# An mLSTM cell and a leaky-ReLU layer in one kernel: weight conversion spread over three engines, a second buffer for exp(a), and a reordered first stage

## The chip, the cores and the metric

The kernel runs on one core of a Trainium2 chip. A core has five instruction streams that run side by side: TensorE (PE in the profile, with its weight loads as PEld), VectorE (DVE), ScalarE (ACT), GpSimd (POOL) and SyncE (SP). SP issues nearly all the DMAs here; ACT issues the few that load the gates. Each stream runs its instructions in order and waits on semaphores for the others. The metric is the device time of one execution in microseconds (us); lower is better.

## The reference, cut to what matters

The first half is a recurrent cell per batch and head (4 x 8 heads, 768 steps, 40 values per head); its output feeds two dense layers with a leaky ReLU between them.

```python
for t in range(S):                                   # S = 768
    m_new  = maximum(f[t] + m, i[t])
    f_stab = exp(f[t] + m - m_new);  i_stab = exp(i[t] - m_new);  m = m_new
    C = f_stab * C + i_stab * outer(v[t], k[t]);     n = f_stab * n + i_stab * k[t]
    y[t] = sigmoid(o[t]) * (C @ q[t]) / maximum(abs(n @ q[t]), 1)
x = y.transpose(0, 2, 1, 3).reshape(3072, 320)
h = x @ w_in                                         # 320 x 2048
out = maximum(0.01 * h, h) @ w_out                   # 2048 x 320
```

Both weight matrices arrive as float64, because the generator scales them by a numpy float64. The other inputs are float32.

## The kernel before, in words

**Chunks and steps.** The 768 time steps are cut into 6 chunks of 128 (NB = 6). A *step* s = 4c + b is one chunk c of one batch b, all 8 heads: 24 steps. Inside a chunk the recurrence is done in matrix form: scores k.q times a decay matrix exp(a[t] + b[s]) below the diagonal, and the state C carries what came before. The dense layers of chunk c, for the 512 tokens of its four batches, are the *ff* work of chunk c.

**A cell step in pieces.** `feed` (L652) loads k and v and spreads the vector a over all partitions into a tile `w` (four buffers), and exp(a) into a tile `ea` (one buffer, L329). `load_blocks` (L306) loads k, q and o a second time into `rb`, laid out for 32x32 transposes. `ahead(s)` (L640) prepares step s: `prep_kq` (transposes of k and q on DVE, L403, and q times exp(a), L409), the loads of k and q for step s + 2, `prep_mask` (POOL adds the causal mask to `w`, L357), `prep_exp` (ACT, eight exps, L365), `prep_vu` (POOL, L384), `prep_o` (ACT, tanh of half the output gate, L392). `u_scores` (L428) is the score matmul and its product with `w` (DVE, L436). `u_mix` (L498) computes the output: matmuls into `pT` (L507, L513), then on DVE a transpose `hb` (L519), the denominators and `xb` (L523), POOL L526, DVE L530, and four DMAs to a scratch `x_dr` in DRAM (L533). `gather_x` (L536) reads it back, transposed, as `xT`, the input of the dense layers.

**The ff work.** `ff_units` gives a list of units: matmuls `ph` (L576) with the relu on ACT (L584) into `acts`, then matmuls `po` (L611), summed over all of `w_out`, with an output copy and DMA. Both `ph` and `po` come out of one pool of four PSUM buffers, so at most two pairs of `ph` are open at once.

**Weights.** The float64 weights come in eight pieces of 1.25 MiB, four of `w_in` and four of `w_out` (QN = 4): `load_weights(n)` (L169) loads piece n into one of two raw buffers (piece 0 into columns of `acts` that are not in use yet), and the generator `narrow_weights(n)` (L197) turns it into float32: an absolute value of the high words on ACT (L209), and on DVE a clamp (L211), an and with a shift (L215), sign and exponent put together (L219), the exponent alone (L221), low word times 2^-52 times that exponent (L223), and a sum (L227). Each `yield` is a place where other work may go in between.

**Order.** PE, DVE, ACT and POOL run in exactly the order in which the program emits their instructions. SP's queue is ordered by the planner of the Tile framework, which follows program order except where it expects a buffer not to be free yet. `first_chunk` (L656) does the cell of chunk 0 and starts the ff work of chunk 0. Then for c = 1 to 6 a loop (L753) runs the ff units of chunk c - 1 and puts the nine cell units of chunk c between them (`u_scores` and `u_mix` for four steps, and `u_gates`, the transposed gates of the next chunk). In pass c = 1 there are 30 ff units, i = 0 to 29: fourteen `ph` units, then sixteen `po` units in which every four need one more piece of `w_out`. There the loop also converts pieces 2 to 7: `todo` (L751) names the unit at which a conversion starts, and each unit then advances it by two yields. The line that places the cell units is

```python
upto = min(n_c, max(0, i + 1 - lead) * n_c // (n_ff - 6 - lead))
```

with lead = 10 in pass 1 and 0 later. In pass 1 that puts `u_scores`, `u_mix`, ... behind units 11, 13, 14, 16, 17, 19, (gates) 20, 22 and 23.

Of the kernel before, what the change touches and what calls it, by code (L numbers as in the profile page):

```python
# [9 lines left out]
F32 = mybir.dt.float32  # L10
# [8 lines left out]
def kernel(  # L19
# [76 lines left out]

    ident = consts.tile([P, P], F32, name="ident")
    make_identity(nc, ident[:])
    zeros = consts.tile([P, P], F32, name="zeros")
    nc.vector.memset(zeros[:], 0.0)  # L100


# [8 lines left out]

    NL = 4
    NR = 2
    kq_t = [consts.tile([P, 2, H, DP], F32, name=f"kq{n}") for n in range(NL)]
    va_t = [consts.tile([P, H, DP], F32, name=f"va{n}") for n in range(NL)]
    rb_t = [consts.tile([P, 3, RW], F32, name=f"rb{n}") for n in range(NR)]
# [52 lines left out]
    def load_weights(n):  # L169

        if n < QN:
            dst = w_in[:, n, :]
        else:
            dst = w_out[:, 4 * (n - QN) : 4 * (n - QN + 1), :].rearrange("p a d -> p (a d)")
        to = dst
        if wide:
            if n == 0:
                raw = acts_l[:, NF * GT - 2 * WC :].bitcast(U64)
            else:
                raw = wk.tile([P, dst.shape[1]], U64, name="raw")[:]  # L180
            raws[n] = (raw, dst)
            to = raw
        if n < QN:
            for r in range(2):
                cols = slice(n * QC + 2 * P * r, n * QC + 2 * P * (r + 1))
                src = moe_w_in[:, cols].rearrange("(k p) c -> p k c", p=DP)
                half = to[DP * r : DP * (r + 1), :].rearrange("p (k c) -> p k c", k=KC)
                at = 0
                while at < KC:
                    k0, n_k = run_of(r, at)  # L190
                    nc.sync.dma_start(half[:, at : at + n_k, :], src[:, k0 : k0 + 2 * n_k - 1 : 2, :])
                    at += n_k
        else:
            rows = moe_w_out[(n - QN) * QC : (n - QN + 1) * QC, :]
            nc.sync.dma_start(to.rearrange("p (a d) -> p a d", d=Dm), rows.rearrange("(a p) d -> p a d", p=P))

    def narrow_weights(n):  # L197

        if not wide:
            return
        raw, dst = raws.pop(n)
        words = raw.bitcast(U32).rearrange("p (c two) -> p c two", two=2)
        lo, hi = words[:, :, 0], words[:, :, 1]
        mt = wk.tile([P, dst.shape[1]], U32, name="wm", bufs=1)
        m = mt[:]
        d = dst.bitcast(U32)
        nc.scalar.activation(dst, hi.bitcast(F32), AF.Abs)  # L209

        nc.vector.tensor_scalar(  # L211
            m.bitcast(F32), dst, scalar1=2.0**-15, scalar2=122879.9921875, op0=ALU.max, op1=ALU.min,
        )
        yield
        nc.vector.tensor_scalar(  # L215
            m, m, scalar1=0x07FFFFFF, scalar2=3, op0=ALU.bitwise_and, op1=ALU.logical_shift_left,
        )
        yield
        nc.vector.scalar_tensor_tensor(d, in0=hi, scalar=0xC0000000, in1=m, op0=ALU.bitwise_and, op1=ALU.bitwise_or)  # L219
        yield  # L220
        nc.vector.tensor_scalar(m, d, scalar1=0xFF800000, scalar2=None, op0=ALU.bitwise_and)  # L221
        yield
        nc.vector.scalar_tensor_tensor(  # L223
            m.bitcast(F32), in0=lo, scalar=2.0**-52, in1=m.bitcast(F32), op0=ALU.mult, op1=ALU.mult,
        )
        yield
        nc.vector.tensor_tensor(dst, dst, m.bitcast(F32), op=ALU.add)  # L227
        yield


    a_dr = dr.tile([NB, 2, BH, P], F32, name="a_dr")
# [4 lines left out]
    def gates(c):  # L236


        m0 = m0s.get(c)
        n = P if c == 0 else BH  # L240
        fc, il = (f0[:], i0[:]) if c == 0 else (fi[c][:, 0, :], fi[c][:, 1, :])
        F = wk.tile([n, P], F32, name="F", bufs=1)
        nc.vector.tensor_tensor_scan(F[:], fc, zeros[:n], 0.0, op0=ALU.add, op1=ALU.add)
        if c > 0:
            il_t = wk.tile([BH, P], F32, name="il", bufs=1)
            nc.vector.tensor_scalar(il_t[:], il, scalar1=m0[:], scalar2=None, op0=ALU.subtract)
            il = il_t[:]
        m = wk.tile([n, P], F32, name="m", bufs=1)
        nc.vector.tensor_tensor_scan(m[:], fc, il, -1e30 if c == 0 else 0.0, op0=ALU.add, op1=ALU.max)
        a = wk.tile([n, P], F32, name="a", bufs=1)  # L250
        nc.vector.tensor_tensor(a[:], F[:], m[:], op=ALU.subtract)
        if c > 0:
            nc.sync.dma_start(a_dr[c, 0], a[:])
        bu = wk.tile([BH, 3, P], F32, name="bu", bufs=1)
        nc.vector.tensor_tensor(bu[:, 0, :], il[:BH], F[:BH], op=ALU.subtract)
        nc.scalar.activation(bu[:, 1, :], bu[:, 0, :], AF.Exp, bias=a[:BH, P - 1 :], scale=1.0)
        nc.scalar.activation(bu[:, 2, :], a[:BH], AF.Exp)
        if c > 0:
            nc.sync.dma_start(a_dr[c, 1], bu[:, 2, :])
            if c + 2 < NB:  # L260
                load_fi(c + 2)
        if c + 1 < NB:
            m1 = wk.tile([BH, 1], F32, name="m0")
            if c == 0:
                nc.vector.tensor_copy(m1[:], m[:BH, P - 1 :])
            else:
                nc.vector.tensor_tensor(m1[:], m0[:], m[:, P - 1 :], op=ALU.add)
            m0s[c + 1] = m1
        return bu, a
# [27 lines left out]

    def load_o(s):
        c, b = divmod(s, B)
        at = NF * GT - 2 * WC - (s + 1) * Dm  # L300
        st[s]["o"] = acts_l[:, at : at + Dm]
        nc.sync.dma_start(
            st[s]["o"].rearrange("p (h d) -> p h d", d=D), o_gate[b, :, ts(c, P), :].rearrange("h p d -> p h d"),
        )
# [18 lines left out]
    def spread(s):  # L323

        c, b = divmod(s, B)
        d = st[s]
        d["w"] = wk.tile([P, H, P], F32, name="w", bufs=NL)
        nc.sync.dma_start(d["w"][:], a_dr[c, 0, b * H : (b + 1) * H, :].partition_broadcast(P))
        d["ea"] = wk.tile([P, PR, P], F32, name="ea", bufs=1)  # L329
        for r in range(2):  # L330
            nc.sync.dma_start(
                d["ea"][DP * r : DP * (r + 1)], a_dr[c, 1, b * H + r : (b + 1) * H : 2, :].partition_broadcast(DP),
            )
# [164 lines left out]
    def u_mix(s):  # L498

        c, b = divmod(s, B)  # L500
        d = st[s]
        if c + 1 < NB:
            state(s)
        pT = psc.tile([P, PR * P], F32, name="pT", tag="c")
# [135 lines left out]
    def ahead(s):  # L640

        if s < NS:
            prep_kq(s)
            if s + NR < NS:
                load_blocks(s + NR, 0)
                load_blocks(s + NR, 1)
            prep_mask(s)
            prep_exp(s)
            prep_vu(s)
            prep_o(s)  # L650

    def feed(s):  # L652
        load(s)
# [80 lines left out]
    with tc.manual_schedule(engines={E.PE, E.DVE, E.Activation, E.Pool}):  # L734
        ffs = first_chunk()
        feed(B)
        for i in range(3):
            load_blocks(B, i)
        load_weights(QN)
        load_weights(QN + 1)  # L740
        feed(B + 1)
        for i in range(3):
            load_blocks(B + 1, i)
        load_weights(QN + 2)
        load_weights(QN + 3)
        feed(B + 2)
        feed(B + 3)


        ffs = ffs[4:6] + ffs[2:4] + ffs[6:]  # L750
        todo = {0: 2, 4: 3, **{9 + 4 * n: QN + n for n in range(4)}}  # L751
        now = iter(())
        for c in range(1, NB + 1):  # L753
            if c > 1:
                ffs = ff_units(c - 1)
            cells = cell_units(c) if c < NB else []
            n_ff, n_c = len(ffs), len(cells)
            lead = 10 if c == 1 else 0
            done = 0
            waiting = []  # L760
            for i in range(n_ff):
                if c == 1:
                    if i in todo:
                        for _ in now:
                            pass
                        now = narrow_weights(todo[i])
                    next(now, None)
                    next(now, None)
                    if i == 8:
                        u_gates(1)  # L770
                        ahead(B)
                if i == lead and c + 1 < NB:
                    bus[c + 1] = gates(c + 1)
                ffs[i]()
                upto = min(n_c, max(0, i + 1 - lead) * n_c // (n_ff - 6 - lead))
                while done < upto:
                    fn, s = cells[done]
                    fn(s)
                    done += 1
                    if fn is u_scores:  # L780
                        ahead(s + 1)
                    elif fn is u_mix:
                        waiting.append(s)
                        if s + NR < NS:
                            load_blocks(s + NR, 2)
                        if s + NL < NS:
                            feed(s + NL)
                if i >= n_ff // 2 - 1:
                    for s in waiting:
                        gather_x(s)  # L790
                    waiting.clear()


# [29 lines left out]
```

## Time and profile before

| What | Value |
|---|---|
| median of 16 runs | 611.89 us (605.89 to 615.09) |
| the profiled execution, its own time | 610.87 us |
| its span, first to last instruction | 609.1 us |
| PE busy | 543.7 us, 89% of the span |
| PEld busy | 369.3 us, 61% |
| DVE busy | 257.2 us, 42% |
| ACT busy | 154.9 us, 25% |
| POOL busy | 110.8 us, 18% |
| mean granted TensorE clock | 0.958 |

Stretches of the span, from the trace: chunk 0 and the start of its ff work run to about 62 us; pass c = 1 from there to 190.8 us; passes 2 to 5 end at about 279, 366, 454 and 537 us; pass 6, which has no cell work, ends the span. A group line gives source line, engine, operation, output and inputs with shapes, count, busy time and mean duration, and the idle time of the engine before them with what ended it. A timeline line gives start, duration, engine, source line, operation, and in brackets the engine's idle time before it. "issue" is time in which an engine waited for nothing that the profile shows.

### The profile page before, as it was taken

Reading aid. Unit: us, or ns where it says so; the run is one execution under the profiler, and the core shown is the slowest. Engines: PE = TensorE matmul, PEld = TensorE weight load, DVE = VectorE, ACT = ScalarE, POOL = GpSimd, SP = SyncE. Lnnn points to the kernel's source line nnn. Section 1 sums busy time; section 2 is a strip of 40 time slices with the busy share of each in tenths; the row PEclk is TensorE's granted clock in tenths of the full one; section 3 lists DMA queues with packets and bytes.
Section 4 is the critical chain, followed back from the end, with each engine's and each line's share of the span. In section 5 each row is a group of like instructions: output and inputs, shape, how many; then the busy total and the mean of one; then the engine's idle time right before and its main releaser. Section 6 shows DMA issues by size and latency. Waiting matters only on the chain.

```text
span 609.1 us, 9093 instructions
## 1 busy us (share of the span) xinstructions
PE 543.7 (89%) x3428; PEld 369.3 (61%) x3428; DVE 257.2 (42%) x423; ACT 154.9 (25%) x401; POOL 110.8 (18%) x128
## 2 busy tenths in 40 slices
PE   5876992978654999999999989999989999999997
PEld 5855782755433756675556766557766567754575
DVE  4756796698830444261445342444403443100000
ACT  4443442420200333113331203331203330012100
POOL 4021520333020122230332030332010110000000
PEclk9998895999785999999999998999999999999999
DMA  9995588744565355653654571563661231100000
GB/s 141 168 175 121 119 259 187 179 159 104 139 164 137 73 136 137 153 137 95 144 134 115 133 173 43 139 150 110 148 171 30 72 87 43 46 22 1 0 23 22
DMA packets 158412, 69.89 MB, mean 115 GB/s; under 512 B 87072, under 2 KB 151200, under 8 KB 158368
## 3 DMA queue, kind: packets, MB, share of 16 engines
q1 hardware_dynamic: 157696, 69.08, 48.1%
q8 instruction: 27, 0.44, 0.3%
q10 hardware_dynamic: 672, 0.23, 0.2%
q14 instruction: 17, 0.14, 0.1%
HBM read 61.90 MB, written 7.37 MB: 114 GB/s over the span
## 4 chain that ended last, share of the span: by engine, by line
PE 70%; DVE 8%; SPq 7%; DMA 6%; issue 5%; ACT 2%; POOL 1%; ACTq 0%; DVEq 0%; POOLq 0%
PE ph L576 32%; PE po L611 28%; PE sc L432 3%; PE pT L513 3%; PE pT L507 3%; SPq L296 3%; DMA rb<-in_k_dram 2%; DMA va<-in_v_dram 2%; SPq L314 1%; DVE kqT L403 1%; PE dC L444 1%; DVE kq L409 1%; DVE wm L223 1%; DVE w L436 1%; DVE wm L221 1%
## 5 line engine op out<-in xcount | busy, mean ns | idle before, releaser
L576 PE MATMUL ph<-xT,w_in 64*128 64x512 f32 (+1 forms) x1120 | 226.2, 553 | 33.8 <-issue 17.8
L611 PE MATMUL po<-w_out,acts 128*128 128x320 f32 x768 | 214.8, 436 | 3.6 <-DVE w_out L227 3.6
L576 PEld LDWEIGHTS ph<-xT,w_in 64*128 64x128 f32 x1120 | 127.0, 197 | 116.8 <-issue 89.8
L611 PEld LDWEIGHTS po<-w_out,acts 128*128 128x128 f32 x768 | 143.5, 190 | 67.4 <-issue 6.0
L584 ACT ACTIVATE acts<-ph 128x512 f32<-128x512 f32 (+1 forms) x112 | 53.7, 532 | 155.7 <-PE ph L576 146.0
L436 DVE TENSOR_TENSOR w<-w,sc 128x512 f32<-128x512 f32 x48 | 30.7, 682 | 147.7 <-PE sc L432 126.6
L365 ACT ACTIVATE w<-w,gT 128x128 f32<-128x128 f32 x192 | 58.5, 393 | 17.4 <-POOL w L357 17.3
L616 ACT COPY y<-po 128x320 f32<-128x320 f32 x24 | 10.2, 425 | 196.0 <-PE po L611 166.5
L455 POOL TENSOR_TENSOR C<-C,gL 64x168 f32<-64x168 f32 x32 | 15.8, 495 | 241.6 <-PE pT L507 240.4
L357 POOL TENSOR_TENSOR w<-w,cmask 128x1024 f32<-128x1024 f32 x20 | 47.5, 2373 | 0.1
L513 PE MATMUL pT<-w,va 128*64 128x128 f32 x320 | 34.5, 280 | 8.3 <-issue 5.8
L403 DVE STREAM_TRANSPOSE kqT<-rb 128x512 f32<-128x512 f32 x40 | 41.0, 1103 | 0.0
L519 DVE STREAM_TRANSPOSE hb<-pT 128x512 f32<-128x512 f32 x20 | 14.3, 715 | 60.5 <-PE pT L513 60.5
L526 POOL TENSOR_TENSOR xb<-xb,den 128x320 f32<-128x320 f32 x20 | 14.6, 728 | 108.3 <-DVE xb L523 93.2
L507 PE MATMUL pT<-kq,C 128*64 128x128 f32 x320 | 34.0, 283 | 0.0
L432 PEld LDWEIGHTS sc<-kqT 40*128 40x128 f32 x384 | 28.4, 205 | 8.2 <-issue 7.6
L409 DVE TENSOR_TENSOR kq<-kqT,ea 40x512 f32<-40x512 f32 x40 | 29.5, 737 | 4.5 <-DMA ea<-a_dr 3.2
L432 PE MATMUL sc<-kqT 40*128 40x128 f32 x384 | 30.7, 297 | 0.0
L513 PEld LDWEIGHTS pT<-w,va 128*64 128x64 f32 x320 | 23.7, 141 | 9.5 <-issue 6.8
L530 DVE STREAM_TRANSPOSE x<-xb 128x512 f32<-128x512 f32 x20 | 22.4, 1118 | 8.3 <-POOL xb L526 8.3
L507 PEld LDWEIGHTS pT<-kq,C 128*64 128x64 f32 x320 | 21.8, 140 | 2.4 <-issue 2.0
L392 ACT ACTIVATE rb<-rb 128x320 f32<-128x320 f32 x20 | 9.3, 465 | 45.5 <-DMA rb<-in_o_gate_dram 37.0
(84 smaller groups left out, 278.8 us busy)
## 6 DMA issues: line engine op xcount, KB each, us to landing
w<-a_dr SPq DMA_DIRECT2D x20, 512.0 KB
rb<-in_k_dram SPq DMA_DIRECT2D x80, 80.0 KB
rb<-in_q_dram SPq DMA_DIRECT2D x80, 80.0 KB
rb<-in_o_gate_dram SPq DMA_DIRECT2D x80, 80.0 KB
ea<-a_dr SPq DMA_DIRECT2D x40, 128.0 KB
raw<-in_moe_w_out_dram SPq DMA_DIRECT2D x4, 1280.0 KB
kq<-in_k_dram SPq DMA_DIRECT2D x24, 160.0 KB
xT<-x_dr SPq DMA_DIRECT2D x40, 96.0 KB
```

Of the source, the lines that this page charges most:

```text
L357: nc.gpsimd.tensor_tensor(w[:], w[:], cmask[:].unsqueeze(1).to_broadcast([P, H, P]), op=ALU.add)
L365: nc.scalar.activation(w[:, h, :], w[:, h, :], AF.Exp, bias=gT[c][:, 0, bh : bh + 1], scale=1.0)
L403: nc.vector.transpose(in_blocks(d["kqT"][:, i]), raw_blocks(s, i, QW).rearrange("p (j n) d -> p j n d", n=TB),)
L409: nc.vector.tensor_tensor(d["qs"][rows], d["kqT"][rows, 1], d["ea"][rows].rearrange("p j t -> p (j t)"), op=ALU.mult,)
L432: nc.tensor.matmul(sc[r][:, j, :], lhsT=kqT[rows, 0, ts(j, P)], rhs=kqT[rows, 1, ts(j, P)], start=True, stop=True,)
L436: nc.vector.tensor_tensor(w[:, r::2, :], w[:, r::2, :], sc[r][:], op=ALU.mult)
L507: nc.tensor.matmul(pT[DP * r : DP * (r + 1), ts(j, P)], lhsT=C[:, b, j, r, :], rhs=d["qs"][:, ts(j, P)], start=True, stop=False,)
L513: nc.tensor.matmul(pT[DP * r : DP * (r + 1), ts(j, P)], lhsT=d["va"][:, h], rhs=d["w"][:, h, :], start=False, stop=True,)
L530: nc.vector.transpose(in_blocks(xq[:]), xb[:].rearrange("p (j n) d -> p j n d", n=TB))
L576: nc.tensor.matmul(ph[r][:, cols], lhsT=w_row(r, slot, j), rhs=xT[DP * r : DP * (r + 1), slot, cols], start=(slot == 0), stop=(slot == KC ...
L584: nc.scalar.activation(acts[:, f, cols], ph[r][:, cols], AF.Prelu, alpha=0.01)
L611: nc.tensor.matmul(po[n][:], lhsT=acts[:, f, ts(n, P)], rhs=w_out[:, f, :], start=(f == 0), stop=(f == NF - 1),)
```

## The change

- **Conversion.** A second ACT instruction turns the low words into float32 times 2^-52, in place in the raw buffer. The product with the exponent and the sum move from DVE to POOL, and stand together as one last part of the generator.
- **Staging.** Piece 1 is also loaded into columns of `acts`, so the two raw buffers serve pieces 2 and 3 first; the o gates of chunk 0 move down to make room. The loads of the four `w_out` pieces are no longer issued before the loop but at units 4, 7, 13 and 17 (`fetch`).
- **exp(a).** `ea` gets two buffers; its DMAs leave `feed` for a function `spread_q`, called two steps ahead from `ahead`. To make room, `zeros` shrinks to one column that is read by broadcast.
- **Order in `ahead` and `u_mix`.** Mask and exps stand ahead of `prep_kq`; the tanh `prep_o` moves from `ahead` to the start of `u_mix`.
- **Placement.** lead is 6 in place of 10, the divisor n_ff - 8 - lead in place of n_ff - 6 - lead: in pass 1 the cell units stand behind units 7, 9, 11, 13, 14, 16, (gates) 18, 20 and 21. `u_gates(1)` and `ahead(4)` come at unit 4 in place of 8, and piece 3's conversion at unit 3 in place of 4.
- **Loads behind gathers.** After a `u_mix`, `gather_x` is emitted ahead of the o loads and the `feed` of later steps.

```diff
-    zeros = consts.tile([P, P], F32, name="zeros")
+    zeros = consts.tile([P, 1], F32, name="zeros")
...
+    EAB = 2
...
-            if n == 0:
-                raw = acts_l[:, NF * GT - 2 * WC :].bitcast(U64)
+            if n < 2:
+                at = NF * GT - 2 * WC * (n + 1)
+                raw = acts_l[:, at : at + 2 * WC].bitcast(U64)
...
+        low = lo.bitcast(F32)
         nc.scalar.activation(dst, hi.bitcast(F32), AF.Abs)
-
+        nc.scalar.activation(low, lo, AF.Copy, scale=2.0**-52)
         nc.vector.tensor_scalar(
             m.bitcast(F32), dst, scalar1=2.0**-15, scalar2=122879.9921875, op0=ALU.max, op1=ALU.min,
         )
...
         nc.vector.tensor_scalar(m, d, scalar1=0xFF800000, scalar2=None, op0=ALU.bitwise_and)
         yield
-        nc.vector.scalar_tensor_tensor(
-            m.bitcast(F32), in0=lo, scalar=2.0**-52, in1=m.bitcast(F32), op0=ALU.mult, op1=ALU.mult,
-        )
-        yield
-        nc.vector.tensor_tensor(dst, dst, m.bitcast(F32), op=ALU.add)
-        yield
+        nc.gpsimd.tensor_tensor(m.bitcast(F32), m.bitcast(F32), low, op=ALU.mult)
+        nc.gpsimd.tensor_tensor(dst, dst, m.bitcast(F32), op=ALU.add)
...
-        d["ea"] = wk.tile([P, PR, P], F32, name="ea", bufs=1)
+
+    def spread_q(s):
+
+        c, b = divmod(s, B)
+        d = st[s]
+        d["ea"] = wk.tile([P, PR, P], F32, name="ea", bufs=EAB)
         for r in range(2):
             nc.sync.dma_start(
                 d["ea"][DP * r : DP * (r + 1)], a_dr[c, 1, b * H + r : (b + 1) * H : 2, :].partition_broadcast(DP),
...
         d = st[s]
+        prep_o(s)
         if c + 1 < NB:
             state(s)
         pT = psc.tile([P, PR * P], F32, name="pT", tag="c")
...
         if s < NS:
+            prep_mask(s)
+            prep_exp(s)
             prep_kq(s)
             if s + NR < NS:
                 load_blocks(s + NR, 0)
                 load_blocks(s + NR, 1)
-            prep_mask(s)
-            prep_exp(s)
+                spread_q(s + NR)
             prep_vu(s)
-            prep_o(s)
...
-        load_weights(QN)
-        load_weights(QN + 1)
         feed(B + 1)
+        spread_q(B + 1)
...
-        load_weights(QN + 2)
-        load_weights(QN + 3)
...
-        todo = {0: 2, 4: 3, **{9 + 4 * n: QN + n for n in range(4)}}
+        todo = {0: 2, 3: 3, **{9 + 4 * n: QN + n for n in range(4)}}
+        fetch = {4: QN, 7: QN + 1, 13: QN + 2, 17: QN + 3}
...
-            lead = 10 if c == 1 else 0
-            done = 0
+            lead = 6 if c == 1 else 0
+            done = fed = 0
...
-                    if i == 8:
+                    if i in fetch:
+                        load_weights(fetch[i])
+                    if i == 4:
                         u_gates(1)
                         ahead(B)
...
-                upto = min(n_c, max(0, i + 1 - lead) * n_c // (n_ff - 6 - lead))
+                upto = min(n_c, max(0, i + 1 - lead) * n_c // (n_ff - 8 - lead))
...
                     elif fn is u_mix:
                         waiting.append(s)
+                if i >= n_ff // 2 - 1:
+                    for s in waiting:
+                        gather_x(s)
+                    waiting.clear()
+                while fed < done:
+                    fn, s = cells[fed]
+                    fed += 1
+                    if fn is u_mix:
                         if s + NR < NS:
                             load_blocks(s + NR, 2)
                         if s + NL < NS:
                             feed(s + NL)
-                if i >= n_ff // 2 - 1:
-                    for s in waiting:
-                        gather_x(s)
-                    waiting.clear()
```

More of the change, by code (lines that the diff above doesn't have):

```diff
@@ L242, in gates @@
         F = wk.tile([n, P], F32, name="F", bufs=1)
-        nc.vector.tensor_tensor_scan(F[:], fc, zeros[:n], 0.0, op0=ALU.add, op1=ALU.add)
+        nc.vector.tensor_tensor_scan(F[:], fc, zeros[:n].to_broadcast([n, P]), 0.0, op0=ALU.add, op1=ALU.add)
         if c > 0:
@@ L299, in load_o @@
         c, b = divmod(s, B)
-        at = NF * GT - 2 * WC - (s + 1) * Dm
+        at = NF * GT - 4 * WC - (s + 1) * Dm
         st[s]["o"] = acts_l[:, at : at + Dm]
@@ L736 @@
         feed(B)
+        spread_q(B)
         for i in range(3):
             load_blocks(B, i)
-        load_weights(QN)
-        load_weights(QN + 1)
         feed(B + 1)
+        spread_q(B + 1)
         for i in range(3):
             load_blocks(B + 1, i)
-        load_weights(QN + 2)
-        load_weights(QN + 3)
         feed(B + 2)
```

## The prediction

> **What bounds the kernel now.** First the page's slices: busy tenths over 40 equal slices of 15.2 us.
>
> ```profile
> PE   5876992978654999999999989999989999999997
> DVE  4756796698830444261445342444403443100000
> POOL 4021520333020122230332030332010110000000
> ```
>
> Up to slice 13 (190 us) PE has holes while DVE is fullest; from there PE is full to the end. The trace by stretches gives PE's share of pass 1 and of a later pass (columns: stretch, length, busy time of PE, PEld, DVE, ACT, POOL, granted clock, DMA share, GB/s):
>
> ```profile
> 60.00:190.00 130.00, 90.29 (x675) 70.11 (x675) 91.28 (x114) 33.66 (x88) 35.87 (x37) 0.85 0.66 165
> 279.00:366.00 87.00, 84.51 (x548) 53.80 (x548) 35.57 (x63) 21.65 (x59) 18.98 (x20) 1.00 0.52 128
> ```
>
> PE's timeline has these gaps after 27 us: 1.95, 2.95, 0.62, 5.00, 0.45 to the start of the loop at 62.5; in pass 1 11.84 (before 104.3), 1.60, 2.23, 2.03, 5.76 (before 158.6) and 15.13 (before 190.8), 38.6 in all; later only 1.18, 2.68 and 1.94 at the starts of passes 3 to 5, together 5.8. So from 190.8 us on only 5.8 us can be won. The rest is pass 1. Its end in the chain of work:
>
> ```profile
> 156.15 2.46 issue
> ...
> 162.48 13.18 PE po L611 x48
> 175.66 15.13 issue
> 190.79 4.60 PE ph L576 x9
> ```
>
> The 15.13 us are no puzzle when SP's queue is read beside them:
>
> ```profile
> 177.34 1.85 SPq L314 DMA_DIRECT2D rb<-in_q_dram  x4
> 179.29 1.48 SPq L533 DMA_DIRECT2D x_dr<-x  x4
> 180.87 1.74 SPq L314 DMA_DIRECT2D rb<-in_o_gate_dram  x4
> 182.70 0.39 SPq L296 DMA_DIRECT2D kq<-in_k_dram  x1
> 183.21 1.41 SPq L296 DMA_DIRECT2D va<-in_v_dram  x2
> 184.67 0.65 SPq L328 DMA_DIRECT2D w<-a_dr  x1
> 185.37 2.54 SPq L547 DMA_DIRECT2D xT<-x_dr  x4
> ```
>
> DVE had the last output of the cell (L530) at 169.7; its store left at 179.3, and the gather stood behind 4.5 us of loads for later steps. The last step's `pT` ended at 162.4: 28.4 us to the next pass.
>
> **What the Trainium skill says.** "SBUF — State Buffer", Who interferes with whom: DVE and GpSimd share a port pair under an exclusive lock; a DVE instruction with two SBUF inputs or in a 2-port mode (`tensor_scalar` among them) and a GpSimd instruction that reads SBUF block each other for the whole instruction. The trace agrees:
>
> ```profile
> 115.81 2.36 POOL L357 TENSOR_TENSOR w<-w,cmask 128x1024 f32<-128x1024 f32 x1
> 118.13 2.01 POOL L384 TENSOR_TENSOR vu<-va,gT 128x336 f32<-128x336 f32 x1
> 116.84 2.67 DVE L219 SCALAR_TENSOR_TENSOR w_out<-raw,wm 128x1280 uint32<-128x1280 uint32 x1
> ```
>
> DVE's L219, 1.49 alone, ends 1.35 after POOL's L357 does; POOL's L384, 0.77 alone, then waits for L219. They take turns. Transposes (L403) and instructions with a PSUM input (L436) don't lose anything beside POOL.
>
> "GPSIMD Engine Reference", 3.1: a two-input float32 `tensor_tensor` takes 4497 ns for 2048 columns against DVE's 2293, 1.96 times. Here L357 takes 2.36 us for 1024 columns. "TensorE: Matmul & The Clock Gate", Part 1: after an idle window of some 3.4 us PE runs at half clock until it has been busy as long. Here the first 32 `ph` after the 15 us gap took 10.15 us, later ones 7.07: 3.1 us.
>
> **The change, part by part.**
>
> *Conversion of one piece.* DVE loses L223 (1.51) and L227 (1.54), 3.05 us, 24 us over eight pieces. ACT gains a pass like L209, 1.37 us; no run shows it, I bound it by 1.0 and 2.0; ACT is 26% busy in pass 1. POOL gains two products of 1280 columns: 2.36/1024 x 1280 = 2.95 each, 5.9 per piece. Bounds: 2.8 (the skill's rate) and 4.0, the slowdown that L496 shows where it met DVE (1.29 on average, 0.72 alone, is 1.8 times). I take 2.95 and count the lock separately. DVE's remaining four (0.83, 0.83, 1.49, 0.83 = 4.0) all take the lock, so a piece now holds the port for 4.0 + 5.9 = 9.9 us in place of 7.0.
>
> *First chunk.* Piece 0's products start when L221 ends at 31.0 and run to 34.0 and 37.2. DVE's denominators of step 1 (L473, L474) and L492 take the lock too: L492 ends at 38.0 in place of 34.1, and the transposes on PE that waited for it start 2.75 later (36.1 to 38.85). PE is dense from there to 56, so all moves by 2.75. Piece 1's products follow POOL's L496 of step 3 (ended 61.1; now about 62.7, since DVE's L223 no longer stands in its way): 62.7 to 68.6. The loop starts at 68.7 in place of 62.5: 6.2 lost.
>
> *Loop, units 0 to 9.* Piece 2's products wait for POOL's memsets (L140, L142; 68.6 to 75.1): 75.1 to 81.0. Piece 3's clamp waits for them; with the mask of step 4 between, piece 3's DVE part ends at 87.4. Behind it stand gT (L280), the exps of step 4 (to 90.2) and, behind those on ACT, the relu of unit 4 (90.8). PE has done units 4 and 5 and waits for PSUM, about 6 us. Piece 3's products (88.7 to 95.3) take turns with L409; mask 5 follows; the scans of `gates(2)` end at 101, its exps on ACT let the next relu go at 103, a second PSUM wait. Units 8 and 9 (5.3 with the clock low) and the `u_mix` of step 4 (2.7) put its `hb` at 111. It was 113.2: what the earlier placement wins, the conversion gives back.
>
> *From one hb to the next.* Now 113.2, 128.8, 146.0, 165.9. After: where a piece's products stand on POOL ahead of a mask (pieces 4 and 6): hb, denominators, xb, POOL L526, L530 3.8; L219 and L221 2.3; products 5.9; one L409 that gets in between 0.75; mask 2.4; exps 2.45; relus 0.7 and the next piece's absolute value 1.4, both behind the exps on ACT; its first two DVE instructions 1.7; sum 21.4, with hand-overs 22. DVE's `hb` is queued behind those two. Piece 5's products come behind their mask: 3.8, mask 2.4, L219 and L221 2.3, L436 and L403 in the products' cover, products 5.9, two L409 1.5: 16. So 111, 133, 149, 171.
>
> *End of pass 1.* From 171: L530 ends at 175; store 1.5 plus 2 to land, gather 2.5 plus 3 (both as at 179.3 to 190.8 now): xT at 184. Piece 7: L219, L221 to 177.6, products to 183.5; units 26 to 29 wait for it: 4 x 4 x 0.28, some at half clock, 5 to 6. Pass 2 starts at 189.5 in place of 190.8: 1.3 won. PE comes to it warm: 3.0 won.
>
> *The moved gathers.* At passes 3 to 5 the gather no longer follows o, k, v and `w` (4.4 us of issue), and the last `u_mix` is two `po` units (2.2) earlier. Gaps of 1.2 to 2.7 vanish: 5.8 won. The cover is the eight `po` units, 9 us; without it the chain L530 to xT of 9 us would show.
>
> *The rest at nothing.* tanh in `u_mix`: it held ACT up to 15.8 us for an o load and so delayed L209; now it has `pT` (1.9) and `hb` (0.7) as cover. `ea`: SP waited 20 us in the window from 60 to 195 for L409 to free it, and the chain went through ea once (3.2 us of DVE); both go, inside the hb distances above. Same number of DMAs. Piece 3 is loaded early, 1.3 MB ahead of step 4's loads, which have until 81. The `fetch` of piece 7 needs the raw buffer that piece 5's product frees at 144, with SP's queue ahead perhaps 163; 1.3 MB at 140 GB/s is 9 us, landing at 172, wanted at 168.5: 0 to 4 us, I take 0. The scan's broadcast column: same two inputs, 0.
>
> *Sum.* Profiled execution 610.87 (span 609.1 and 1.8 around it) - 1.3 - 3.0 - 5.8 = 600.8. It ran 1.0 under the median of the runs, so 601.8; I say 601.
>
> **Rivals.**
>
> *Cover is better than my queue count.* DVE and POOL seldom meet, ACT's absolute values get through before the exps, every hb distance is 16 and the first hb comes a few us earlier. For it: DVE sheds 18 us in pass 1, where it was 70% busy with waits; ACT's holds of 9.8 and 15.8 go. Against: the order above is fixed. hb of step 7 at 157 to 159, pass 2 from 176: 588.
>
> *Slower: POOL's products are the bound.* At 4.0 each: 2 per piece on pieces 0 and 1, which stand on the path, 2 on pieces 2 and 3 where exps wait, 2 on each of 4 to 7: 14 us, and piece 7's load 3.5. Pass 2 from 204: about 616. For it: L496's 1.8 times. Against: L357 and L384 keep their 2.3 ns per column in most places. It decides from a start of pass 2 beyond 201.5.
>
> *The change wins nothing.* The planner puts the gathers behind the loads as before, and pass 1 ends at 190 to 193: 611. For it: the planner sorts SP, not the program. Against: program order is what it follows when buffers are free.
>
> **How the numbers follow.** A measurement of this kernel can tell about 0.3% (1.8 us) from no change. Chances: my forecast 0.50 (594 to 609), better cover 0.25 (583 to 594), slower 0.17 (614 to 622), nothing 0.08 (609 to 614). Range 584 to 614: it leaves out the far tenth of the slow case and the edge of the fast one. Faster 0.76, same 0.07, slower 0.17.
>
> **What would show it.** Right: POOL's new products near 2.95 each, more where DVE meets them; the loop's first `ph` of unit 0 near 69; `hb` near 111, 133, 149, 171; the gather directly behind its store on SP; no PE gap over 1 us at passes 3 to 5. Wrong: PE holes in pass 1 that stay below 20 us in all, or `po` units that wait for the last piece beyond 190.

## The result, and the profile after

The changed kernel takes 606.65 us (median, 604.08 to 607.72) against 612.44 of the kernel before (median of 48 runs): ratio 0.9904, interval 0.9881 to 0.9926. It is faster by 1%, as forecast in sign and half as much as forecast in size. Of all executions below, one was slow, the profiled one of experiment 5 (788.88 us at a granted clock of 0.649), and it is left out together with its profile. The changed kernel's profiled execution took 604.33, near the low end of its runs; its span is 602.5, 6.6 less than before. Line numbers below are those of the changed kernel: `hb` is L524, the products of the conversion L226 and L227 on POOL, q times exp(a) L413, the mask L361, the exps L369, the absolute value L212, `po` L616, `ph` L581.

The page's slices, now of 15.1 us each:

```profile
PE   5868558969806999999999999999999999999997
...
DVE  4765368979655355270555342543504442100000
...
POOL 4060875565715033330133030332200120000000
```

PE has holes up to slice 13, and in slice 12 (166 to 181 us) it now does next to nothing. POOL works at 5 to 8 tenths from slice 5 to slice 11, where it was at 0 to 3 for the most part. Behind slice 13 PE is full without a break. The same two stretches as before (length, busy time of PE, PEld, DVE, ACT, POOL, granted clock, DMA share, GB/s):

```profile
60.00:190.00 130.00, 85.85 (x652) 67.34 (x653) 93.26 (x104) 39.50 (x91) 78.08 (x51) 0.83 0.64 158
279.00:366.00 87.00, 87.00 (x562) 53.73 (x562) 35.63 (x63) 22.55 (x61) 18.99 (x20) 1.00 0.53 133
```

In the first of the two, pass 1, POOL went from 35.87 to 78.08 us busy. DVE went from 91.28 to 93.26, and over the whole span from 257.2 to 258.8, though the eight conversions shed 3.05 us of DVE work each, 24 in all: what DVE lost in work came back in other records that grew longer. PE did less in these 130 us (85.85 against 90.29). In the later stretch PE is busy for all 87.00.

The chain of work at the end of pass 1 (start, length, what):

```profile
176.11 3.43 issue
179.54 2.92 POOL wm L226
182.54 2.89 POOL w_out L227
185.47 11.57 PE po L616 x32
197.04 7.07 PE ph L581 x32
```

Where the chain before had 15.13 us of "issue" in front of `ph`, it now runs through the last conversion on POOL and then through the last four `po` units. Pass 2 starts at 197.0; it was 190.8. SP's queue there:

```profile
161.70 0.38 SPq L197 DMA_DIRECT2D raw<-in_moe_w_out_dram  x1
...
177.25 1.46 SPq L538 DMA_DIRECT2D x_dr<-x  x4
178.81 0.80 SPq L313 DMA_DIRECT2D rb<-in_o_gate_dram  x2
180.01 2.53 SPq L552 DMA_DIRECT2D xT<-x_dr  x4
182.58 1.07 SPq L313 DMA_DIRECT2D rb<-in_o_gate_dram  x2
```

The gather (L552) now follows its store (L538) with only two small loads between them, and the loads for later steps come behind it: what the edit was written to do. It didn't shorten pass 1, because the dense layers had another thing to wait for by then.

From the start of pass 2 to the last matmul the kernel took 415.7 us before and takes 402.9 now. So the span's 6.6 is 12.8 won in passes 2 to 6 less 6.2 lost ahead of pass 2. Of these 6.2, 5.2 were lost before the loop: its unit 0 starts at 67.8 in place of 62.5. Pass 1 itself takes 129.2 in place of 128.3. PE's gaps in it add up to 37.2 us where they were 38.6: they changed place more than size, and the last is now 19.0 us long.

### The profile page after: what moved, and what is told of

It is laid out like the page before. It is cut to its first block, busy times and chain, and to the rows that moved or that the text cites. A ratio compares the mean times of both kernels' runs of the same rounds, so it can differ in the third digit from the quotient of the medians.

```text
span 602.5 us, 9126 instructions
## 1 busy us (share of the span) xinstructions
PE 538.6 (89%) x3428; PEld 354.8 (59%) x3428; DVE 258.8 (43%) x407; ACT 164.4 (27%) x409; POOL 157.2 (26%) x144
## 4 chain that ended last, share of the span: by engine, by line
PE 69%; POOL 1%; issue 1%; ACT 0%; ACTq 0%; POOLq 0%
PE po L616 31%; PE ph L581 29%; PE sc L436 3%; PE pT L512 2%; PE pT L518 2%; PE dC L448 1%; POOL wm L226 0%; POOL w_out L227 0%; PE tg L273 0%; PE tg L274 0%; ACT y L621 0%; ACTq L621 0%; POOLq L388 0%
## 5 line engine op out<-in xcount | busy, mean ns | idle before, releaser
L616 PE MATMUL po<-w_out,acts 128*128 128x320 f32 x768 | 218.1, 443 | 27.4 <-POOL w_out L227 21.8
L581 PE MATMUL ph<-xT,w_in 64*128 64x512 f32 (+1 forms) x1120 | 220.2, 545 | 14.7 <-ACT acts L589 9.1
L616 PEld LDWEIGHTS po<-w_out,acts 128*128 128x128 f32 x768 | 146.5, 193 | 91.6 <-POOL w_out L227 23.1
L581 PEld LDWEIGHTS ph<-xT,w_in 64*128 64x128 f32 x1120 | 111.6, 195 | 105.9 <-issue 93.8
L369 ACT ACTIVATE w<-w,gT 128x128 f32<-128x128 f32 x192 | 58.5, 393 | 43.1 <-POOL w L361 35.6
L361 POOL TENSOR_TENSOR w<-w,cmask 128x1024 f32<-128x1024 f32 x20 | 48.6, 2429 | 0.0
L413 DVE TENSOR_TENSOR kq<-kqT,ea 40x512 f32<-40x512 f32 x40 | 43.3, 1083 | 1.3
L524 DVE STREAM_TRANSPOSE hb<-pT 128x512 f32<-128x512 f32 x20 | 14.3, 716 | 55.0 <-PE pT L518 54.9
L518 PE MATMUL pT<-w,va 128*64 128x128 f32 x320 | 31.7, 273 | 0.8 <-DVE w L440 0.8
L512 PE MATMUL pT<-kq,C 128*64 128x128 f32 x320 | 32.1, 277 | 0.0
L518 PEld LDWEIGHTS pT<-w,va 128*64 128x64 f32 x320 | 20.9, 137 | 1.3 <-DVE w L440 1.3
L512 PEld LDWEIGHTS pT<-kq,C 128*64 128x64 f32 x320 | 19.7, 137 | 2.4 <-issue 2.4
L226 POOL TENSOR_TENSOR wm<-wm,raw 128x1280 f32<-128x1280 f32 x6 | 17.7, 2956 | 13.0 <-issue 8.6
```

Source lines behind the costliest of these rows:

```text
L361: nc.gpsimd.tensor_tensor(w[:], w[:], cmask[:].unsqueeze(1).to_broadcast([P, H, P]), op=ALU.add)
L369: nc.scalar.activation(w[:, h, :], w[:, h, :], AF.Exp, bias=gT[c][:, 0, bh : bh + 1], scale=1.0)
L413: nc.vector.tensor_tensor(d["qs"][rows], d["kqT"][rows, 1], d["ea"][rows].rearrange("p j t -> p (j t)"), op=ALU.mult,)
L512: nc.tensor.matmul(pT[DP * r : DP * (r + 1), ts(j, P)], lhsT=C[:, b, j, r, :], rhs=d["qs"][:, ts(j, P)], start=True, stop=False,)
L518: nc.tensor.matmul(pT[DP * r : DP * (r + 1), ts(j, P)], lhsT=d["va"][:, h], rhs=d["w"][:, h, :], start=False, stop=True,)
L581: nc.tensor.matmul(ph[r][:, cols], lhsT=w_row(r, slot, j), rhs=xT[DP * r : DP * (r + 1), slot, cols], start=(slot == 0), stop=(slot == KC ...
```

## The experiments

Each kernel was run beside the kernel before, whose medians there were 613.2 to 613.5 us; ratios are against that, with their intervals. Three marks of the profile are followed through: "unit 0" is the start of the loop's first `ph` on PE; "hb" is the DVE transpose that follows the matmuls of a `u_mix`, so the four hbs of pass 1 are those of steps 4 to 7; "pass 2" is the start of its first `ph`.

**1. Conversion on DVE again, in the changed kernel**

```diff
-        nc.scalar.activation(low, lo, AF.Copy, scale=2.0**-52)
-        nc.gpsimd.tensor_tensor(m.bitcast(F32), m.bitcast(F32), low, op=ALU.mult)
-        nc.gpsimd.tensor_tensor(dst, dst, m.bitcast(F32), op=ALU.add)
+        nc.vector.scalar_tensor_tensor(
+            m.bitcast(F32), in0=lo, scalar=2.0**-52, in1=m.bitcast(F32), op0=ALU.mult, op1=ALU.mult,
+        )
+        yield
+        nc.vector.tensor_tensor(dst, dst, m.bitcast(F32), op=ALU.add)
+        yield
```

> The changed kernel with the conversion of the kernel before (no low-word pass on ACT, product and sum back on DVE, six yields), all else as changed. Theory (the POOL half is what costs in pass 1, the rest of the change wins): unit 0 starts near 62.5 in place of 67.8, the first hb of pass 1 comes near 94 to 100 in place of 107.8, the next ones 15 to 17 apart, pass 2 starts between 158 and 176 in place of 197.0, and the time is 568 to 588. Rival (DVE is what is short in pass 1, and taking 3 us per piece off it is what lets the cell units stand earlier): hb distances of 18 and more, pass 2 not before 197, time 606 or more.

Measured: 592.24 us, ratio 0.9683 (0.9631 to 0.9735). Unit 0 at 62.1; hb at 97.9, 115.3, 130.9 and 160.9; pass 2 at 182.1. The first three hbs are as the theory had them, 17.4 and 15.6 apart. The fourth is 30 behind the third, and the reason stands on ACT's timeline:

```profile
157.88 1.35 ACT L211 ACTIVATE w_out<-raw 128x1280 f32<-128x1280 f32 x1 [15.17 <-DMA raw<-in_moe_w_out_dram]
```

ACT waited 15.17 us for the load of piece 7. So two things hold pass 1: the POOL half, whose absence is worth 14 us here, and the load of piece 7.

**2. The conversion over three engines alone, in the kernel before** (the conversion's lines of the change, nothing else)

> The kernel before with the conversion over three engines alone. Theory: unit 0 starts 5 to 6 us later (68), the first hb comes later by as much or more, pass 2 starts 8 to 25 us after 190.8 and the time is 620 to 637. Rival (relief for DVE): pass 2 starts before 190.8, time below 610.

Measured: 624.09 us, ratio 1.0186 (1.0140 to 1.0231). Unit 0 at 67.6 in place of 62.5, first hb at 123.4 in place of 113.2, pass 2 at 202.4 in place of 190.8:

```profile
202.38 3.42 PE L574 MATMUL ph<-xT,w_in 64*128 64x512 f32 x6 [17.76 <-issue]
```

By itself this part costs 11 us: 5.0 arise before unit 0, 5.1 more up to the first hb, 1.5 behind the last one (176.0). Between the first and the last hb nothing is lost or won in this order (52.6 us, 52.7 before), so the relief for DVE doesn't show in the sum.

**3. The gathers ahead of the loads alone, in the kernel before** (the last hunk of the change)

> The kernel before with one edit, the gathers emitted ahead of the loads for later steps. Theory: the store and gather of step 7 leave SP 3 to 6 us earlier, pass 2 starts at 185 to 188 in place of 190.8; the gaps at passes 3 to 5 (5.8 us) go, and most of the half-clock start behind them (2); time 597 to 602. Rival (the planner of SP's queue keeps the old order, or the gathers wait for something else): time 610 to 613, the gaps stay.

Measured: 601.21 us, ratio 0.9817 (0.9776 to 0.9859). The gaps at passes 3 to 5 are gone. The idle time before pass 2 fell from 15.13 to 8.71, with xT still what ends it:

```profile
188.64 7.90 PE L576 MATMUL ph<-xT,w_in 64*128 64x512 f32 x20 [8.71 <-DMA xT<-x_dr]
```

Pass 2 began 2.2 earlier though the last hb came 4.1 later in this execution (170.0 against 165.9). One part out of six wins 11 to 12 us, twice what the whole change wins.

**4. Piece 7 fetched at unit 15 in place of 17, in the changed kernel**

```diff
-        fetch = {4: QN, 7: QN + 1, 13: QN + 2, 17: QN + 3}
+        fetch = {4: QN, 7: QN + 1, 13: QN + 2, 15: QN + 3}
```

In the changed kernel this load sets the last hb. ACT's timeline there, absolute value of piece 7 behind the exps of step 8:

```profile
160.32 2.45 ACT L369 ACTIVATE w<-w,gT 128x128 f32<-128x128 f32 x8 [21.38 <-POOL w L361]
170.31 1.35 ACT L212 ACTIVATE w_out<-raw 128x1280 f32<-128x1280 f32 x1 [7.54 <-DMA raw<-in_moe_w_out_dram]
```

The raw buffer was free when L226 of piece 5 ended at 139.3; the load left SP at 161.7, behind stores, gathers and the loads of two steps.

> The changed kernel with piece 7 of the weights fetched at unit 15 in place of 17, so ahead of the store, gather and loads that follow step 6. Theory (ACT waited 7.5 us at 170.3 for this load, and hb of step 7 and the last conversion stood behind that): the load leaves SP near 143 to 150 in place of 161.7, hb of step 7 comes at 165 to 167 in place of 173.4, pass 2 starts at 188 to 191 in place of 197.0, time 598 to 601. Rival (something else is as late, the mask of step 8 or the conversion itself): pass 2 moves by less than 2, time 604 to 607.

Measured: 597.11 us, ratio 0.9751 (0.9710 to 0.9792). The load left at 153.1, the last hb came at 167.5, pass 2 started at 190.4. ACT went straight from the exps to the absolute value:

```profile
162.05 2.44 ACT L369 ACTIVATE w<-w,gT 128x128 f32<-128x128 f32 x8 [21.37 <-POOL w L361]
164.40 1.34 ACT L212 ACTIVATE w_out<-raw 128x1280 f32<-128x1280 f32 x1
```

The load left later than I had expected, behind the first two gathers, and was still in time. From hb of step 6 to hb of step 7 it is 22.0 us now: the distance that the forecast had worked out for a loop without this wait.

**5. Both together: conversion on DVE, piece 7 fetched at unit 14**

```diff
-        fetch = {4: QN, 7: QN + 1, 13: QN + 2, 17: QN + 3}
+        fetch = {4: QN, 7: QN + 1, 13: QN + 2, 14: QN + 3}
```

(beside the edit of experiment 1)

> The changed kernel with the conversion on DVE again and piece 7 fetched at unit 14. With the fetch at 17 ACT waited 15.2 us for piece 7 at 157.9 and hb of step 7 came 30 us behind the one before, at 160.9. Theory (that load and the POOL half are the two things that hold pass 1): piece 7's load leaves SP between 130 and 140, hb of step 7 comes at 145 to 149, the last sum of piece 7 ends before 160, pass 2 starts at 165 to 172, time 575 to 583. Rival (the load only hid another wait, such as the mask of step 8 or the gather): hb of step 7 at 155 or later, time 587 or more.

Measured: 579.52 us, ratio 0.9447 (0.9394 to 0.9499), the best of all, 5.5% under the kernel before. Whether its hbs and pass 2 came where expected is not shown, since it has no profile to go with these times; experiment 7 differs from it by the ACT pass and by the form of the product on DVE, and has one. Ahead of experiment 3 it is by 22 us; placement, staging, the second buffer and the order in `ahead` stand between the two, and which of them wins how much is not taken apart.

**6. Pieces 0 and 1 on DVE, the other six over three engines, in the changed kernel** (the two branches chosen by `n > 1`)

> The changed kernel with pieces 0 and 1, those of the first chunk, converted wholly on DVE, pieces 2 to 7 as changed. Theory (their POOL half stands on the path to unit 0 and everything in pass 1 hangs on what came before): unit 0 at 62.5 in place of 67.8, the hbs of pass 1 all 4 to 6 earlier, pass 2 at 191 to 193 in place of 197.0, time 600 to 603. Rival (later waits take it up): hb of step 7 moves by less than 2, time 605 to 607.

Measured: 598.68 us, ratio 0.9768 (0.9718 to 0.9817). hb at 101.4, 122.2, 137.4 and 168.1, each 5.2 to 6.3 earlier than in the changed kernel, pass 2 at 191.6, 5.4 earlier. Unit 0 starts at 61.9 in place of 67.8: these 5.9 us, POOL's share before the loop, go through to pass 2 all but undiminished. The time is a little better than expected.

**7. The ACT pass kept, product and sum on DVE, fetch at 14**

```diff
-        nc.gpsimd.tensor_tensor(m.bitcast(F32), m.bitcast(F32), low, op=ALU.mult)
-        nc.gpsimd.tensor_tensor(dst, dst, m.bitcast(F32), op=ALU.add)
+        nc.vector.tensor_tensor(m.bitcast(F32), m.bitcast(F32), low, op=ALU.mult)
+        yield
+        nc.vector.tensor_tensor(dst, dst, m.bitcast(F32), op=ALU.add)
+        yield
```

> The changed kernel with the ACT pass over the low words kept, but product and sum on DVE, and piece 7 fetched at unit 14: of the three engines only POOL is taken out. Theory (the POOL half is what costs; the ACT pass is free): as the kernel with the whole conversion on DVE and the fetch at 14, 577 to 583; unit 0 near 62.5, first hb 95 to 100, distances 15 to 19, pass 2 at 168 to 174. Rival (the extra pass on ACT, 1.4 per piece ahead of relus and exps, costs its share too): 584 to 592.

Measured: 580.98 us, ratio 0.9483 (0.9446 to 0.9520), whose interval overlaps that of experiment 5. hb at 98.4, 115.6, 131.2 and 150.3, pass 2 at 171.5. The pass on ACT costs nothing that can be seen; it is POOL that costs. Set against experiment 4, which has the POOL half and piece 7 in time too, pass 2 comes 18.9 us earlier: 3.9 of them arise before unit 0, 7.2 from there to the first hb, 6.0 between the hbs and 1.8 behind the last.

**8. The tanh back in the preparation of a step, in the changed kernel** (`prep_o(s)` moved from `u_mix` to the end of `ahead`)

> The changed kernel with the tanh of the output gate back at the end of the preparation of a step instead of the start of its mix. Theory (on ACT it waits for the o load and holds what follows): ACT waits for the o load before L396 by 5 us or more at a time in pass 1 and the absolute values of pieces 5 to 7 come later, pass 2 starts 3 to 12 us later than 197.0, time 609 to 618. Rival (the o loads now come in time, or other waits cover it, as the forecast had it): time 605 to 608.

Measured: 607.22 us, ratio 0.9894 (0.9847 to 0.9941), that of the changed kernel (0.9904) within its interval. The wait that the theory needs is not there: in pass 1 ACT waits before no tanh (L396) for an o load (the longest idle time before one is 1.60, for DVE). With the loads ordered as they are now, o comes in time. Pass 2 came at 199.7 in its profile, 2.7 later, but the changed kernel's profile is of an execution near the low end of its runs; by the times this part of the change is worth nothing in it.

**9. One buffer for exp(a) in place of two, in the changed kernel** (`EAB = 1`)

> The changed kernel with one buffer for exp(a) in place of two, its issue two steps ahead left as it is. The forecast put the second buffer at nothing beyond the hb distances. Theory (SP waits again for L413 before it can send the next ea, 15 us or more in pass 1, and other transfers stand behind): pass 2 0 to 6 later than 197.0, passes 3 to 6 as before, time 606 to 613. Rival (the wait has no one behind it that matters): 605 to 608, pass 2 within 1 of 197.

Measured: 629.10 us, ratio 1.0278 (1.0242 to 1.0314). The theory was right in kind, but expected far too little. SP's waits from 60 to 220 us (in total, times, longest) and ACT's wait for piece 7:

```profile
SPq L335 <- DVE kq L413: 45.0, 4, 24.9
```

```profile
196.08 1.35 ACT L212 ACTIVATE w_out<-raw 128x1280 f32<-128x1280 f32 x1 [24.25 <-DMA raw<-in_moe_w_out_dram]
```

The DMA for the ea of step s + 2 waits until L413 of step s + 1 is done, and SP's whole queue waits with it, piece 7's load too: last hb at 199.1, pass 2 at 221.6. The second buffer and the issue two steps ahead belong together: with the early issue and one buffer the changed kernel is slower than the kernel before.

**10. The placement of the kernel before, in the changed kernel**

```diff
-            lead = 6 if c == 1 else 0
+            lead = 10 if c == 1 else 0
-                upto = min(n_c, max(0, i + 1 - lead) * n_c // (n_ff - 8 - lead))
+                upto = min(n_c, max(0, i + 1 - lead) * n_c // (n_ff - 6 - lead))
-                    if i == 4:
+                    if i == 8:
```

(and piece 3 from unit 4)

> The changed kernel with the placement of the kernel before (lead 10, divisor with 6, gates and preparation of step 4 at unit 8, piece 3 from unit 4). Theory (the earlier placement is what makes up for part of the conversion's cost in pass 1): the first hb at 115 to 124 in place of 107.8, pass 2 at 201 to 208 in place of 197.0, time 610 to 618; no gap at passes 3 to 5 all the same, since the gathers stand ahead of the loads. Rival (with the port short it doesn't matter where the units stand): pass 2 within 2 of 197, time 605 to 608.

Measured: 602.31 us, ratio 0.9807 (0.9750 to 0.9865). Theory and rival were both wrong: neither allowed for a time below 605, and this kernel is faster than the changed one. The first hb came at 123.6, as late as expected, but the last at 175.4, 2.0 behind the changed kernel's, and pass 2 at 187.1, 11.7 behind that hb where the changed kernel needs 23.6. With `u_mix` of step 7 at unit 23, piece 7's DVE part and products (done at 174.0) stand ahead of it in their queues; with it at unit 21 they stand behind. Part of this comes back at once: ACT's output copies wait for a `y` buffer whose store is queued on SP, and PE stands still for 3.3 us at 192.7 (bracket: idle time and what ended it):

```profile
182.23 0.43 ACT L621 COPY y<-po 128x320 f32<-128x320 f32 x1 [1.73 <-PE po L616]
195.50 0.83 ACT L621 COPY y<-po 128x320 f32<-128x320 f32 x2 [12.84 <-DMA out_dram<-y]
```

By the profiles the two kernels' spans are 1.3 us apart, by the ratios 1%. That packing the cell units tighter wins nothing in the changed kernel is shown; how much it costs is not settled.

**11. Piece 7 fetched at 14 and converted from unit 19, in the changed kernel**

```diff
-        todo = {0: 2, 3: 3, **{9 + 4 * n: QN + n for n in range(4)}}
+        todo = {0: 2, 3: 3, 9: QN, 13: QN + 1, 17: QN + 2, 19: QN + 3}
```

> The changed kernel, POOL half included, with piece 7 fetched at unit 14 and its conversion started at unit 19 in place of 21, so that its products are issued ahead of the mix of step 7. With the fetch alone moved (to 15) the last hb came at 167.5 and pass 2 at 190.4, 23 later. Theory (the last conversion behind the last hb makes that distance): pass 2 starts 10 to 14 after the last hb, at 182 to 187, time 588 to 594. Rival (what holds the end is the store, the gather and the half clock, or the conversion only changes places with the hb): pass 2 at 189 or later, time 596 or more.

Measured: 594.86 us, ratio 0.9711 (0.9680 to 0.9742). The result lies between theory and rival: the last hb moved back to 172.2 (ACT waited 8.36 for the load again, ahead of it now), and pass 2 came at 187.9, 15.7 behind the hb in place of 22.9. The order at the end is worth some 2 to 3 us beside experiment 4, not the 7 that the distance alone shows.

**12. Conversions on DVE started at 9, 12, 15 and 18** (beside the edits of experiment 5, and piece 6 fetched at 11)

> The kernel with the whole conversion on DVE and the fetch at 14, its last four conversions started at units 9, 12, 15 and 18 in place of 9, 13, 17 and 21, piece 6 fetched at 11 in place of 13. Theory (at the end of pass 1 the last conversion stands behind hb of step 7 on DVE, and the last four po units behind it): with its DVE part ahead of that hb pass 2 waits for xT alone and starts 10 to 14 after the last hb, 4 to 8 earlier than without; time 571 to 577. Rival (the conversions only push the cell's DVE work back by as much): 578 to 582.

Measured: 580.90 us, ratio 0.9488 (0.9454 to 0.9522): no gain over experiment 5. hb at 98.3, 117.9, 135.3 and 156.0, pass 2 at 172.8. The rival held: beside experiment 7 the end is 4.3 shorter (16.8 from the last hb to pass 2, 21.2 there), but the last hb comes 5.7 later.

## Why the prediction was right or wrong

| Step | Forecast | Measured |
|---|---|---|
| POOL's two products | 2.95 each | 2.96 and 2.88 to 2.98 |
| ACT pass | 1.37 | 1.40 |
| unit 0 of the loop | 68.7 | 67.8 |
| relu of unit 4 done | 90.8 | 91.1 |
| `hb` of steps 4 to 7 | 111, 133, 149, 171 | 107.8, 128.5, 143.7, 173.4 |
| last product done | 183.5 | 185.4 |
| pass 2 | 189.5 | 197.0 |
| won in passes 2 to 6 | 8.8 | 12.8 |
| time | 601 | 606.65 |

**The time came near the forecast partly by luck.** Two errors of opposite sign stand behind it. Pass 2 was to start 1.3 us earlier than before and started 6.2 later; passes 2 to 6 won 4.0 more than forecast. What the change does before the loop was forecast well (6.2 lost, 5.2 measured). The loop of pass 1 was to get 7.5 shorter and got 0.9 longer: here the forecast had the wrong sign.

**The mechanism of the cost was right.** POOL's half takes turns with DVE on the port and stands ahead of the mask, so the exps, the relus and the next absolute value wait behind it. The trace shows it where the forecast put it. POOL's timeline, then DVE's, at piece 3:

```profile
88.30 2.94 POOL L226 TENSOR_TENSOR wm<-wm,raw 128x1280 f32<-128x1280 f32 x1
91.32 3.22 POOL L227 TENSOR_TENSOR w_in<-w_in,wm 128x1280 f32<-128x1280 f32 x1
94.49 2.80 POOL L361 TENSOR_TENSOR w<-w,cmask 128x1024 f32<-128x1024 f32 x1
```

```profile
89.57 5.51 DVE L413 TENSOR_TENSOR kq<-kqT,ea 40x512 f32<-40x512 f32 x2
95.11 2.46 DVE L242 TENSOR_TENSOR_SCAN F<-fi,zeros 32x128 f32<-32x128 f32 x1
```

DVE's two L413, 1.4 us together where POOL is quiet, last 5.51: one waits for each product. The scan L242 then waits for the mask. Over the whole kernel, DVE's product with exp(a) and ACT's exps before (L409, L365), then after (L413, L369), and the new product:

```profile
L409 DVE TENSOR_TENSOR kq<-kqT,ea 40x512 f32<-40x512 f32 x40 | 29.5, 737 | 4.5 <-DMA ea<-a_dr 3.2
L365 ACT ACTIVATE w<-w,gT 128x128 f32<-128x128 f32 x192 | 58.5, 393 | 17.4 <-POOL w L357 17.3
...
L413 DVE TENSOR_TENSOR kq<-kqT,ea 40x512 f32<-40x512 f32 x40 | 43.3, 1083 | 1.3
L369 ACT ACTIVATE w<-w,gT 128x128 f32<-128x128 f32 x192 | 58.5, 393 | 43.1 <-POOL w L361 35.6 <-DVE gL L280 7.5
...
L226 POOL TENSOR_TENSOR wm<-wm,raw 128x1280 f32<-128x1280 f32 x6 | 17.7, 2956 | 13.0 <-issue 8.6 <-ACT acts L589 3.5 <-ACT w L369 0.8
```

L413 averages 1083 ns; the same instruction before averaged 737. Over 40 of them that alone is 13.8 us of DVE. The exps idled 17.3 us for the mask before and 35.6 now; in experiment 7, with the order of the change but no products on POOL, it is 10.5. Experiments 1 and 2 show the cost from both sides (14 us the one way, 11 the other), experiment 7 that it is POOL and not ACT, experiment 6 that the share before the loop runs through to pass 2.

How the cost divides between the turns on the port and the mask behind the products can be read in part from the distances between the hbs. They are 20.8, 15.2 and 22.0 us in experiment 4, with the products on POOL, and 17.2, 15.6 and 19.1 in experiment 7, without. In the second distance, and only there, the products (piece 5's) follow the mask on POOL. It is the one that isn't longer, though DVE's two L413 wait for the products there too (4.1 us together, 1.6 in experiment 7). Experiment 2 agrees: between its hbs no mask stands directly behind products (the next one starts 2 us or more after they end), and nothing is lost there. So between the hbs it is the place ahead of the mask that costs, and not the turns on the port. For the 7.2 us between unit 0 and the first hb no run separates the two.

**Sizes that were off.** Pass 2 came 7.5 us later than forecast, from two terms.

- *Piece 7's load.* The forecast said 0 to 4 us and took 0. ACT waited 7.54. The three hbs before had come 3 to 5 earlier than forecast, so the load was late against an earlier need, and the last hb came out 2.4 later. Experiment 4 takes the wait away and gives the forecast's own 22.
- *The last four `po` units.* "4 x 4 x 0.28, some at half clock, 5 to 6" counted sixteen instructions. Each matmul stands in the profile twice (768 `po` records for 384), so it is 32, and 8.7 us at full clock (64 took 17.42 later). After a PE gap of 19.0 us they took 11.6, at a mean granted clock of 0.76. This is the larger term, 5.6: by estimate 4.2 of it from the misread count, which the page shows, and 1.3 from more time at half clock than was put in.

**Passes 2 to 6 won more than forecast**, 12.8 against 5.8 for gaps and 3.0 for one start at half clock. PE's idle time in them fell by 5.9 and its busy time by 7.0 (409.4 to 402.4). Of the 7.0, 3.1 is the start of pass 2, at half clock before (granted 0.50 from 190.7 to 196.0), as forecast. The forecast priced no other start; it had taken from the Trainium skill ("TensorE: Matmul & The Clock Gate", Part 1) that it needs an idle window of some 3.4 us. The trace doesn't agree: the gap of 2.68 us before pass 4 had such a price too. The start of pass 4 in the chain before, then after:

```profile
366.38 8.91 PE ph L576 x32
...
364.79 7.07 PE ph L581 x32
```

The mean granted clock was 0.64 from 366.3 to 371.0 before; this is 1.8. Behind the gap of 1.94 before pass 5 the clock was full. The remaining 2.1 is spread over the passes and not explained.

**What was put at nothing.** The tanh: right by the times of experiment 8, though not by the cover that I named; the o loads simply came in time. ea: nothing with two buffers; experiment 9 shows a loss of 22 us behind that nothing if the second buffer is missing, which the forecast didn't name. Placement: I wrote that what the earlier placement wins the conversion gives back, at hb of step 4. That hb did gain (107.8 against 123.6 in experiment 10), but nothing of it was left at pass 2: the tighter order also put the last conversion behind the last `u_mix` on DVE and POOL, and the forecast, which has both in this order in its sum, didn't ask what the old order gave there.

**Rivals.** Better cover occurred in small part (the first three hbs 3 to 5 us early), and pass 2 shows nothing of it; the times near 580 needed the conversion off POOL. POOL's products at 4.0 each didn't occur either: their records stay at 2.9 to 3.2, and it is DVE's records that grow. That the planner leaves the gathers behind the loads was wrong. It kept two of the four o loads ahead of them and no more.

## What to carry to other kernels

Before work goes from a busy engine to an idle one, look at what the two share and at what is queued behind the new work: here 24 us of work left DVE, DVE stayed as busy as before (257.2 and 258.8), and the kernel lost 11 to 14 us. When a change has many parts, look for the part that acts on the queue: putting the gather ahead of loads that nobody waits for yet won 11 to 12 us alone, and a fetch two units earlier 9 to 10. Add up the winning and losing stretches separately: a total that fits can hide two errors, as it did here. Count records and instructions before you multiply: a float32 matmul stood twice in this profile.

## What the runs showed of the hardware that I had not expected

- Where POOL and DVE contend, nearly all of the wait shows in the duration of DVE's records: L413 up to 3.28 us for one (0.74 alone), while POOL's products stay at 2.88 to 2.98 with one of 3.22. A POOL that looks undisturbed can be what stretches DVE.
- POOL's memsets, which read nothing, ran longer beside DVE too: the pair of L143 beside DVE's L214 and L218 took 2.23 us where pairs elsewhere took 1.07, and L218 took 1.11 in place of 0.83.
- A gap of only 2.68 us on PE was followed by matmuls at a reduced clock (granted 0.64 from 366.3 to 371.0 before the change; the first 32 `ph` of pass 4 took 8.91 in place of 7.07), a gap of 1.94 us was not (granted 1.00 from 454.4 to 460.0).
